# Attention with a routed expert layer: weight casts under one condition of two engines, staging block picked by register

## The chip, the cores and the metric

The kernel runs on one core of a Trainium2 chip. The metric is the device time of one execution in microseconds, as a median over runs. The engines are TensorE (PE, with its weight loads PEld), VectorE (DVE), ScalarE (ACT), GpSimd (POOL) and SyncE (SP). SP only issues transfers and conditions. A "q" behind an engine's name (SPq, ACTq, DVEq) means its sequencer: waits, branches, issues.

## The reference

```python
scores = scale * np.matmul(q, k.transpose(0, 1, 3, 2)) - np.log(S)      # 8 x 12 heads, 448 x 64
attn_out = np.matmul(1.0 / (1.0 + np.exp(-scores)), v)
x = attn_out.transpose(0, 2, 1, 3).reshape(B * S, H * D)                # 3584 tokens x 768
expert_idx = argmax(cosine(x, expert_emb) / tau)                         # 8 experts
for e in range(E):
    mask = expert_idx == e
    h = np.maximum(x[mask] @ w1[e], 0.0)                                 # 768 -> 1024
    out[mask] = gate_w[mask, None] * (h @ w2[e])                         # 1024 -> 768
```

Each token goes to one expert alone. How many tokens an expert gets is known only at run time.

## The kernel before, in words

The first part is attention over 48 head pairs, with the routing worked out beside it. The second part, which the change touches, is the expert layer. The tokens are sorted by expert into tiles of 128 rows, the fullest expert first. Two early tiles of that expert (-2 and -1) run ahead of the loop, which then goes over tiles `t = 0 ..`, at most `MAXL`; tiles past the last are skipped.

A tile has its rows gathered by POOL (`gather`, L1019) and transposed by a transfer of SP (`xt`, L1021). `layer1` is 36 matmuls against w1 (L200; L206 when the tile holds at most 64 tokens). `hidden` takes the result out on ACT (L259) and DVE (L261) and transposes it by two transfers of SP (`hT`, L263). `layer2` is 48 matmuls against w2 (L212; L219 for 64 tokens or fewer), `evac2` scales the output (L903, L905), and POOL scatters it (L1048). The loop runs `layer1` one tile ahead of `layer2`.

Weights come from memory in float32 and are used as two float16 parts. ACT writes the high part of a chunk (`high`, L160), DVE subtracts it from the float32 value for the low part (`low`, L164). w1 has 6 chunks of 128 x 1024, w2 has 8 of 128 x 768. There is one set of float16 tiles, `wts`. The float32 chunks lie in one of two stages, 0 or 1, by the expert's rank: the second expert uses stage 1, the third stage 0, and so on. The stages are separate tiles per chunk (`stages[stage][which][c]`); in the trace the first four w1 chunks of stage 0 are called `stage`, all others `s_w`.

`cast(u, which)` casts the weights if a new expert begins at tile `u`. The table `ci[:, 0]` holds 0 for no cast, 1 or 2 for a cast from stage 0 or 1. For ACT and then for DVE it goes through both stages, each under a condition of its own (L989), so there are two conditions on each engine in a call, ACT's for stage 1 standing ahead of DVE's for stage 0. w1 is cast two tiles ahead of the expert's first tile, behind `layer1(t + 1)`, w2 one tile ahead, behind `layer2(t)`. `fetch(u, n)` issues part `n` of 4 of the weights of the expert after next into the stage that `cast` has freed, again with one condition for each stage (L979), on SP. The calls for one expert are spread over four rounds of the loop, in the order in which SP issues transposes too.

Order: ACT, SP and POOL, and PE and DVE, keep the order of the program in the loop (`manual_schedule`). The last `hT` ahead of the loop, of tile -1, is the one that the planner places on SP by itself. The second expert's w1 (six transfers of 512 KB) is fetched beside the last two head pairs, its w2 ahead of and in round 0; the third expert's four parts are fetched in rounds 0, 0, 1 and 2.

```python
for en in (ET.Activation, ET.DVE):
    for st in range(2):
        with tc.If(regs[en, u] == 1 + st):
            weight_steps(None, which, range((NKC, NFC)[which]), st)[1 + (en == ET.DVE)]()
```

Of the kernel before, what the change touches and what calls it, by code (L numbers as in the profile page):

```python
# [12 lines left out]
F32 = mybir.dt.float32  # L13
I32 = mybir.dt.int32
AF = mybir.ActivationFunctionType
ALU = mybir.AluOpType
# [5 lines left out]
P = 128  # L22
# [7 lines left out]
E = 8  # L30
# [15 lines left out]
GC = P * JG  # L46
MAXL = (NT - (GS + 1) * GC // E + (E - 1) * (P - 1)) // P + 2
MINL = NJ - NE
# [58 lines left out]
def attn_moe_kernel(ctx: ExitStack, tc: tile.TileContext, q, k, v, emb, tau, w1, w2, consts, eye, out, dbg=None):  # L107
# [3 lines left out]
    dpool = ctx.enter_context(tc.tile_pool(name="dpool", bufs=1, space=DRAM))  # L111
    stg = ctx.enter_context(tc.tile_pool(name="stg", bufs=4))
    ps_s = ctx.enter_context(tc.tile_pool(name="ps_s", bufs=2, space=PSUM))
# [30 lines left out]

    stages = [[None] * 2, [None] * 2]

    def weight_steps(e, which, chunks, stage=None):
        src, w, i = (w1, F, 0) if which == 0 else (w2, DM, 2)
        tiles = [stg.tile([P, F], F32, name="stage")[:, :w] if stage is None else stages[stage][which][c] for c in chunks]

        def fetch():
            for c, s in zip(chunks, tiles):
                nc.sync.dma_start(s, src[bass.ds(e, 1), c * P:(c + 1) * P, :].rearrange("o p f -> (o p) f"))

        def high():
            for c, s in zip(chunks, tiles):
                if stage is None:
                    nc.vector.tensor_scalar(wts[i][:, c, :], s, SW, None, op0=ALU.mult)
                else:
                    nc.scalar.activation(wts[i][:, c, :], s, AF.Copy, scale=SW)  # L160

        def low():
            for c, s in zip(chunks, tiles):
                nc.vector.scalar_tensor_tensor(wts[i + 1][:, c, :], s, SW, wts[i][:, c, :], op0=ALU.mult, op1=ALU.subtract)  # L164

        return fetch, high, low
# [107 lines left out]
    with ExitStack() as actx:  # L274
# [271 lines left out]
        def choose(c):  # L546
# [19 lines left out]
            yield 1.0  # L566
            nc.vector.scalar_tensor_tensor(least, eoh, 2.0, eoh2, op0=ALU.mult, op1=ALU.add)
            nc.vector.scalar_tensor_tensor(rank0, least, 512.0, cs("desc"), op0=ALU.mult, op1=ALU.add)
# [111 lines left out]
        with tc.manual_schedule(engines={ET.SP, ET.PE, ET.Activation, ET.DVE, ET.Pool}):  # L680
            for i in range(NPAIR):
# [62 lines left out]
                if er:  # L744
                    while wq and len(wp) < 2 + 2 * (i + 6 > NPAIR):
                        fetch_next()
                    if i + 2 >= NPAIR:
                        for c in range(3 * (i + 2 - NPAIR), 3 * (i + 3 - NPAIR)):
                            weight_steps(er[1], 0, [c], 1)[0]()
                if i == 0:  # L750
# [6 lines left out]
                if i + 3 == NPAIR:  # L757
                    mctx.close()
                    ps_m.append(mctx.enter_context(tc.tile_pool(name="ps_m", bufs=2, space=PSUM)))
                    qctx.close()  # L760
                    bw = ctx2.enter_context(tc.tile_pool(name="bw", bufs=1, side="right", reuse_waits="tile"))
                    bp2 = ctx2.enter_context(tc.tile_pool(name="bp2", bufs=2, side="right", reuse_waits="tile"))
                    stages[1][0] = [bw.tile([P, F], F32, name=f"s1_w1_{c}") for c in range(NKC)]
                if i == 0:
# [151 lines left out]
    with tc.issue_after(six_op.ins):  # L916
# [24 lines left out]
        nc.vector.scalar_tensor_tensor(pr, pr, -2.0, kp[:, 1:], op0=ALU.mult, op1=ALU.add)  # L941
        to = bp1.tile([P, MAXL], F32, name="to")
        nc.vector.tensor_scalar(to, pr, 1.0, None, op0=ALU.add)
        vd = bp1.tile([P, MAXL], F32, name="vd")
# [9 lines left out]
        nc.vector.tensor_tensor(hm[:, NE:], hm[:, NE:], vd, op=ALU.mult)  # L954
        nc.vector.tensor_scalar(pr, hm[:, NE:], 2.0, -4.0, op0=ALU.mult, op1=ALU.add)
        nc.vector.tensor_tensor(pr, pr, vd, op=ALU.mult)
        ci = bp1.tile([P, 4, MAXL], I32, name="ci")
        nc.vector.tensor_scalar(ci[:, 2], pr, 4.0, None, op0=ALU.add)
        nc.vector.tensor_tensor(ci[:, 0], ca, to, op=ALU.mult)
        nc.vector.scalar_tensor_tensor(ch, nx, some[:, 0:1], ch, op0=ALU.is_lt, op1=ALU.mult)  # L960
        nc.vector.tensor_tensor(ci[:, 3], ch, to, op=ALU.mult)
        pos = bp1.tile([P, E], F32, name="pos")
# [8 lines left out]
    def fetch(u, n):  # L971
        if u and not 2 <= u < MAXL:
            return
        if u not in regs:
            regs[u] = (nc.values_load(ci[0:1, 3, u:u + 1], engines=[ET.SP], min_val=0, max_val=2),
                       nc.values_load(ci[0:1, 1, u:u + 1], engines=[ET.SP], min_val=0, max_val=E - 1))
        to, e = regs[u]
        for st in range(2):
            with tc.If(to == 1 + st):  # L979
                weight_steps(e, *PARTS[n], st)[0]()  # L980

    def cast(u, which):
        if not 2 <= u < MAXL:
            return
        for en in (ET.Activation, ET.DVE):
            if (en, u) not in regs:
                regs[en, u] = nc.values_load(ci[0:1, 0, u:u + 1], engines=[en], min_val=0, max_val=2)
            for st in range(2):
                with tc.If(regs[en, u] == 1 + st):  # L989
                    weight_steps(None, which, range((NKC, NFC)[which]), st)[1 + (en == ET.DVE)]()  # L990

# [3 lines left out]
    for w in wp:  # L995
        for f in w[1:]:
            f()
    man.enter_context(tc.manual_schedule(engines={ET.Activation, ET.SP, ET.Pool}))
    layer2_full([hT.pop((-2, half)) for half in range(2)], po[0])
    evac2(-2, po[0], bp1.tile([P, DM], F32, name="obe"))  # L1000
    rest = token_rest()
    next(rest)
    with tc.tile_pool(name="xr2", bufs=4, reuse_waits="tile") as xr2:
        nrm[:] = xr2, nc.vector
        for f in later:
            f()
    xctx.close()
    bp4 = ctx2.enter_context(tc.tile_pool(name="bp4", bufs=1, reuse_waits="tile"))
    stages[1][1] = [bp4.tile([P, DM], F32, name=f"s1_w2_{c}") for c in range(NFC)]
    stg2 = ctx2.enter_context(tc.tile_pool(name="stg2", bufs=1, reuse_waits="tile"))  # L1010
    stages[0] = [[stg.tile([P, F], F32, name="stage") for c in range(4)] + [stg2.tile([P, F], F32, name=f"s0_w1_{c}") for c in range(4, NKC)],
                 [stg2.tile([P, DM], F32, name=f"s0_w2_{c}") for c in range(NFC)]]
    bp3 = ctx2.enter_context(tc.tile_pool(name="bp3", bufs=3, reuse_waits="tile"))
# [28 lines left out]
    def scatter(t):  # L1042
# [3 lines left out]
        for d in range(2):  # L1046
            with (wide if d else guard)(ET.Pool, t):  # L1047
# [6 lines left out]
                stored.append(ins)  # L1054

    stored = []
    gather(0)
# [4 lines left out]
    for t in range(1, 3):  # L1062
        gather(t)
    layer1(0, xg_t.pop(0))
    weight_steps(er[1], *PARTS[2], 1)[0]()
    ends = ctx.enter_context(ExitStack())
    for t in range(MAXL):
# [9 lines left out]
        if t == 0:  # L1077
# [6 lines left out]
            nc.vector.memset(po[1][1], 0.0)  # L1084
            weight_steps(er[1], *PARTS[3], 1)[0]()
            fetch(0, 0)
        elif t < 3:
            fetch(0, 1 + t)
        if t > 1:
            fetch(t, 2)  # L1090
            fetch(t - 1, 3)
        cast(t + 2, 0)
        layer2(t)
        if t == 0:
            fetch(0, 1)
        fetch(t + 2, 0)
# [27 lines left out]
```

## Time and profile before

| | |
|---|---|
| median of 3 runs (lowest to highest) | 931.33 us (931.27 to 934.27) |
| the profiled execution, its own time | 925.67 us |
| span of the profile, first to last instruction | 923.8 us |
| PE busy in the span | 796.5 us (86%) |
| mean granted TensorE clock | 0.937 of full speed |

The profiled execution is 5.66 us shorter than the median; sums are made against it. In the lists of instructions a row gives start, duration, engine, source line, operation, tiles written and read, shape and count; in brackets stands how long the engine had been idle before, and what ended that.

### The profile page before, as it was taken

The page shows a single profiled execution, that of the slowest core. Times are in us where ns is not written, and L with a number is a line of the kernel's source. Part 1 is how long each engine was busy: PE and PEld are TensorE (multiplying, and loading weights), DVE is VectorE, ACT ScalarE, POOL GpSimd, SP SyncE. Part 2 cuts the span into 40 slices and gives each one's busy share as a digit, 9 for nine tenths or more (in the row PEclk, how much of TensorE's full clock was granted, in tenths as well). Part 3 has the DMA queues.
Part 4 walks back from the last instruction along what each step waited for, and adds up shares of the span by engine and source line. Part 5 has one row for each costly group of instructions (what it writes and reads, how often), then busy time and mean ns, then how long its engine had stood idle before and what let it go on. Part 6 is the DMA issues. An engine that isn't in the chain of part 4 may idle for free.

```text
span 923.8 us, 18744 instructions
## 1 busy us (share of the span) xinstructions
PE 796.5 (86%) x5847; PEld 382.5 (41%) x5847; DVE 372.7 (40%) x713; ACT 372.9 (40%) x551; POOL 198.1 (21%) x249
## 2 busy tenths in 40 slices
PE   6999999999998749987998998799995979566593
PEld 2344444444443325543454543355442435232351
DVE  3544575876784742201331112314323134303541
ACT  5777777777886030102221130313313213321530
POOL 2123523433431210311212110121120202011011
PEclk9999999999999979999999997899998889797798
DMA  8477979997987982976687655665788666677221
GB/s 209 116 174 179 239 182 235 272 233 202 217 237 168 225 177 44 294 212 157 181 213 165 133 114 144 180 199 114 190 205 179 145 208 166 174 170 157 60 49 41
DMA packets 243231, 160.80 MB, mean 174 GB/s; under 512 B 184748, under 2 KB 222102, under 8 KB 243024
## 3 DMA queue, kind: packets, MB, share of 16 engines
q1 hardware_dynamic: 233728, 123.29, 58.2%
q0 software_dynamic: 8880, 35.12, 11.9%
q8 instruction: 69, 1.13, 0.5%
q14 instruction: 138, 1.13, 0.4%
q10 hardware_dynamic: 416, 0.13, 0.1%
HBM read 96.69 MB, written 22.81 MB: 129 GB/s over the span
## 4 chain that ended last, share of the span: by engine, by line
issue 37%; DMA 13%; POOL 3%; POOLq 2%; another core or an unknown queue 0%
DMA xg<-xs,gix 9%; DMA out<-ob,six 4%; POOL xg L1019 2%; POOL out L1048 1%; POOLq L241 1%; POOLq L1047 0%; POOLq L1048 0%; POOLq L1018 0%; POOLq L1019 0%; POOLq L1069 0%; POOLq _compat.py:109 0%
## 5 line engine op out<-in xcount | busy, mean ns | idle before, releaser
L200 PE MATMUL pss<-w,xt 128*128 128x512 f16 x900 | 208.4, 390 | 37.0 <-DVEq L989 20.2
L212 PEld LDWEIGHTS <-hT 128*128 128x128 f16 x1296 | 132.6, 103 | 167.0 <-issue 52.2
L376 ACT ACTIVATE att<-pss,bias_s 128x896 f32<-128x896 f32 x144 | 139.8, 1005 | 32.0 <-PE pss L374 26.6
L200 PEld LDWEIGHTS <-xt 128*128 128x128 f16 x900 | 89.4, 100 | 150.2 <-issue 54.0
L1048 POOL DMA_INDIRECT out<-ob,six x58 | 58.6, 1010 | 433.7 <-ACTq L989 349.9
L212 PE MATMUL psa<-w,hT 128*128 128x384 f16 x624 | 114.2, 347 | 37.4 <-DMA hT<-hr 21.3
L212 PE MATMUL pso<-w,hT 128*128 128x384 f16 x672 | 122.3, 345 | 25.4 <-DVEq L989 11.9
L259 ACT ACTIVATE hr<-pss 128x512 f16<-128x512 f32 x60 | 35.4, 594 | 233.2 <-PE pss L200 155.1
L403 PE MATMUL psa<-att,vt 128*64 128x448 f32 x576 | 125.4, 556 | 0.0
L261 DVE SCALAR_TENSOR_TENSOR hr<-pss,hr 128x512 f16<-128x512 f32 x60 | 41.1, 689 | 197.4 <-ACT hr L259 180.1
L164 DVE SCALAR_TENSOR_TENSOR w<-s_w,w 128x768 f16<-128x768 f32 (+1 forms) x86 | 83.9, 1043 | 85.1 <-ACT w L160 62.0
L374 PE MATMUL pss<-kq 64*128 64x448 f16 x864 | 100.3, 356 | 2.2 <-ACT att L376 1.3
L160 ACT ACTIVATE w<-s_w 128x768 f16<-128x768 f32 (+1 forms) x86 | 70.9, 904 | 51.7 <-SPq L979 49.9
L341 POOL COPY pk<-qk 128x384 f32<-128x384 f32 x93 | 45.5, 516 | 141.9 <-PE ptr L353 75.4
L364 DVE SCALAR_TENSOR_TENSOR kq<-ptr,kq 128x448 f16<-128x448 f32 x96 | 59.8, 624 | 26.5 <-ACT kq L361 24.0
L374 PEld LDWEIGHTS <-kq 64*128 64x128 f16 x864 | 35.2, 95 | 75.6 <-issue 52.0
L363 DVE TENSOR_SCALAR kq<-ptr 128x448 f16<-128x448 f32 x70 | 43.4, 620 | 41.9 <-PE ptr L353 41.8
L403 PEld LDWEIGHTS psa<-att,vt 128*64 128x64 f32 x576 | 34.9, 136 | 60.7 <-issue 50.2
L428 DVE SCALAR_TENSOR_TENSOR xT<-psa,xT 128x384 f16<-128x384 f32 x96 | 32.9, 384 | 34.9 <-PE pss L374 25.7
L903 ACT ACTIVATE ob<-psa,own 128x384 f32<-128x384 f32 x16 | 9.3, 579 | 80.5 <-PE psa L212 62.4
L456 POOL TENSOR_TENSOR xf<-xrow 128x768 f32<-128x768 f16 x24 | 39.8, 1658 | 8.5 <-ACT xq L461 8.1
L164 DVE SCALAR_TENSOR_TENSOR w<-stage,w 128x1024 f16<-128x1024 f32 (+1 forms) x26 | 29.1, 1147 | 27.7 <-DMA xt<-xg 14.6
(212 smaller groups left out, 546.9 us busy)
## 6 DMA issues: line engine op xcount, KB each, us to landing
s_w<-in_moe_w SPq DMA_DIRECT2D x56, 384.0 KB
s_w<-in_moe_w SPq DMA_DIRECT2D x30, 512.0 KB
qk<-in_q SPq DMA_DIRECT2D x48, 192.0 KB
qk<-in_k SPq DMA_DIRECT2D x48, 192.0 KB
vt<-in_v SPq DMA_DIRECT2D x48, 192.0 KB
xs<-xrow POOLq DMA_DIRECT2D x24, 384.0 KB
stage<-in_moe_w SPq DMA_DIRECT2D x18, 512.0 KB
stage<-in_moe_w SPq DMA_DIRECT2D x8, 384.0 KB
```

Of the source, the lines that this page charges most:

```text
L160: nc.scalar.activation(wts[i][:, c, :], s, AF.Copy, scale=SW)
L164: nc.vector.scalar_tensor_tensor(wts[i + 1][:, c, :], s, SW, wts[i][:, c, :], op0=ALU.mult, op1=ALU.subtract)
L200: nc.tensor.matmul(ph[half][:, t % 2], xt[:, xi, kc, :], wts[wi][:, kc, half * HF:(half + 1) * HF], start=(n == 0), stop=(n == len(L1_TERM ...
L212: nc.tensor.matmul(po[d][:, :HD], hs[fc // 4][:, i, fc % 4, :], wts[wi][:, fc, d * HD:(d + 1) * HD], start=(n == 0), stop=(n == len(L2_TER ...
L261: d = nc.vector.scalar_tensor_tensor(hr[:, 1], ps, 0.0, hr[:, 0], op0=ALU.max, op1=ALU.subtract)
L341: en.tensor_copy(t.rearrange("p c h d -> p h c d"), qk[i][:, j])
L363: nc.vector.tensor_scalar(hi, x, SQK, None, op0=ALU.mult)
L364: nc.vector.scalar_tensor_tensor(lo, x, SQK, hi, op0=ALU.mult, op1=ALU.subtract)
L374: nc.tensor.matmul(ps[:, h, :S], x[r, ki, c * P:(c + 1) * P], x[r, qi, QC], start=(n == 0), stop=(n == 2))
L376: nc.scalar.activation(a, ps[:, :, :S], AF.Sigmoid, bias=bias_s, scale=1.0 / (8.0 * SQK * SQK))
L403: nc.tensor.matmul(accumulator(i)[h * D:(h + 1) * D, :S], vv[i][:, h, c, :], a[:, h, :], start=((i % 2 == 1 or i == 0) and c == 0), stop=( ...
L1048: ins = nc.gpsimd.indirect_dma_start(out.rearrange("n (h d) -> (n h) d", h=2), bass.IndirectOffsetOnAxis(ap=six[:, d, c:c + 1], axis=0), o ...
```

## The change

`cast` now has two conditions in a call, one for each half of the matrix's chunks, and each holds the work of both engines, ACT's and DVE's in turn chunk by chunk. The stage is no longer a Python constant with an arm for each value: both stages of a chunk are one tile `[P, 2, F]`, and the stage is an index in a register. `fetch` has one condition instead of two in the same way. The tables hold 2 for "nothing", 0 or 1 for the stage. The fullest expert gets at least 4 tiles in the loop instead of 2 (`LEAST`), and `MAXL` grows by 2. The fetch of the second expert's w1 leaves the end of the attention: its first part is issued on SP just ahead of `layer2(-2)`, the second ahead of `layer1(0)`, its w2 in rounds 0 and 1. The third expert's parts move to round 2 (parts 0 and 1), 3 and 4.

```diff
-MAXL = (NT - (GS + 1) * GC // E + (E - 1) * (P - 1)) // P + 2
+MAXL = (NT - (GS + 1) * GC // E + (E - 1) * (P - 1)) // P + LEAST      # LEAST = 4
+    def block(stage, which, c):
+        return stages[which][c][:, stage] if isinstance(stage, int) else stages[which][c][:, bass.ds(stage, 1)].rearrange("p o f -> p (o f)")
-                    if i + 2 >= NPAIR:
-                        for c in range(3 * (i + 2 - NPAIR), 3 * (i + 3 - NPAIR)):
-                            weight_steps(er[1], 0, [c], 1)[0]()
-                    stages[1][0] = [bw.tile([P, F], F32, name=f"s1_w1_{c}") for c in range(NKC)]
+                    stages[0][:3] = [bw.tile([P, 2, F], F32, name=f"s_w1_{c}") for c in range(3)]
...
     def fetch(u, n):
-        if u and not 2 <= u < MAXL:
+        if u and not LEAST <= u < MAXL:
...
-        for st in range(2):
-            with tc.If(to == 1 + st):
-                weight_steps(e, *PARTS[n], st)[0]()
+        with tc.If(to < 2):
+            weight_steps(e, *PARTS[n], nc.s_assert_within(to, 0, 1))[0]()
     def cast(u, which):
...
+        at, n = regs["c", u], (NKC, NFC)[which] // 2
+        for half in range(2):
+            with tc.If(at < 2):
+                now = nc.s_assert_within(at, 0, 1)
+                for c in range(half * n, half * n + n):
+                    for f in weight_steps(None, which, [c], now)[1:]:
+                        f()
...
     man.enter_context(tc.manual_schedule(engines={ET.Activation, ET.SP, ET.Pool}))
+    weight_steps(er[1], *PARTS[0], 1)[0]()
     layer2_full([hT.pop((-2, half)) for half in range(2)], po[0])
...
+    ahead(1)
     layer1(0, xg_t.pop(0))
-    weight_steps(er[1], *PARTS[2], 1)[0]()
...
-            weight_steps(er[1], *PARTS[3], 1)[0]()
-            fetch(0, 0)
-        elif t < 3:
-            fetch(0, 1 + t)
+        if t < 2:
+            ahead(2 + t)
+        elif t in (2, 4):
+            fetch(0, 0 if t == 2 else 3)
+        if t:
+            fetch(t, 2)
         if t > 1:
-            fetch(t, 2)
             fetch(t - 1, 3)
         cast(t + 2, 0)
         layer2(t)
-        if t == 0:
-            fetch(0, 1)
+        if t in (2, 3):
+            fetch(0, t - 1)
```

`ahead(n)` is `weight_steps(er[1], *PARTS[n], 1)[0]()`. The small table operations of VectorE ahead of the loop are rewritten for the new codes (two more of them).

## Rows read from the trace of the kernel before

**Rows 1.** Stretches with casts: busy time (PE, PEld, DVE, ACT, POOL), granted clock, DMA.

```profile
440.00:480.00 40.00, 37.88 (x215) 18.86 (x214) 15.08 (x19) 11.75 (x18) 8.15 (x8) 0.98 0.79 204
...
540.00:600.00 60.00, 47.54 (x233) 23.93 (x232) 19.32 (x22) 16.39 (x22) 6.66 (x7) 0.86 0.56 149
```

**Rows 2.** Waits of PE, whole span: sum in us, times, longest.

```profile
PE psa L212 <- DMA hT<-hr: 21.3, 3, 9.8
PE pss L200 <- DVEq L989: 20.2, 4, 6.6
```

**Rows 3.** Timeline of PE: two undisturbed layers, then six layers behind casts.

```profile
535.93 7.93 PE L200 MATMUL pss<-w,xt 128*128 128x512 f16 x36
543.70 7.96 PE L212 MATMUL psa<-w,hT 128*128 128x384 f16 x48
...
558.89 10.32 PE L200 MATMUL pss<-w,xt 128*128 128x512 f16 x35 [6.62 <-DVEq L989]
...
590.71 9.69 PE L212 MATMUL psa<-w,hT 128*128 128x384 f16 x46 [5.61 <-DVEq L989]
...
716.54 10.01 PE L200 MATMUL pss<-w,xt 128*128 128x512 f16 x35 [6.62 <-DVEq L989]
...
748.04 9.53 PE L212 MATMUL pso<-w,hT 128*128 128x384 f16 x46 [5.60 <-DVEq L989]
...
840.42 9.51 PE L200 MATMUL pss<-w,xt 128*128 128x512 f16 x35 [6.41 <-DVEq L989]
...
868.96 10.50 PE L212 MATMUL pso<-w,hT 128*128 128x384 f16 x46 [6.33 <-DVEq L989]
```

**Rows 4.** Timeline of ACT and DVE, the third expert's w1 (stage 0).

```profile
546.01 3.90 ACT L160 ACTIVATE w<-stage 128x1024 f16<-128x1024 f32 x4 [0.53 <-ACT hr L259]
...
551.88 4.63 DVE L164 SCALAR_TENSOR_TENSOR w<-stage,w 128x1024 f16<-128x1024 f32 x4 [5.50 <-ACTq L989]
```

**Rows 5.** Timeline of ACT, DVE and PE, the fourth expert's w1 (stage 1).

```profile
639.00 5.79 ACT L160 ACTIVATE w<-s_w 128x1024 f16<-128x1024 f32 x6 [1.52 <-SPq L979]
...
640.09 6.90 DVE L164 SCALAR_TENSOR_TENSOR w<-s_w,w 128x1024 f16<-128x1024 f32 x6 [1.88 <-ACT w L160]
...
643.28 8.23 PE L200 MATMUL pss<-w,xt 128*128 128x512 f16 x36
```

**Rows 6.** Waits of SP's own queue, whole span.

```profile
SPq L979 <- SPq L979: 87.8, 83, 5.7
```

**Rows 7.** The fetch conditions' line: its branches (ns min/median/max), who waited for it.

```profile
L979 SPq COMPARE_BRANCH  x268: 2/45/692, 382.2 to 917.7; - x134
...
  ACT w L160: 59.6, 10
```

**Rows 8.** Timeline of PE: two layers behind late casts.

```profile
800.49 0.80 PE L212 MATMUL psa<-w,hT 128*128 128x384 f16 x2 [10.31 <-ACT w L160]
...
833.43 0.58 PE L200 MATMUL pss<-w,xt 128*128 128x512 f16 x1 [9.93 <-ACTq L989]
```

**Rows 9.** Timeline of SP, end of attention; then PE, early tiles' second layers.

```profile
292.70 2.39 SPq L153 DMA_DIRECT2D s_w<-in_moe_w  x3
...
300.21 15.67 SPq L444 DMA_TRANSPOSE xrow<-xT  x4
...
325.09 9.72 PE L212 MATMUL psa<-w,hT 128*128 128x384 f16 x48 [8.11 <-DMA hT<-hr]
344.63 10.18 PE L212 MATMUL psa<-w,hT 128*128 128x384 f16 x48 [9.83 <-DMA hT<-hr]
```

**Rows 10.** Timeline of PE, rounds 2 to 5: the second expert's casts.

```profile
407.46 9.50 PE L212 MATMUL psa<-w,hT 128*128 128x384 f16 x48 [3.39 <-DMA hT<-hr]
...
423.12 9.65 PE L212 MATMUL pso<-w,hT 128*128 128x384 f16 x48 [2.15 <-DMA hT<-hr]
...
436.11 0.38 PE L200 MATMUL pss<-w,xt 128*128 128x512 f16 x1 [3.34 <-ACT w L160]
...
460.11 0.48 PE L212 MATMUL pso<-w,hT 128*128 128x384 f16 x2 [0.69 <-ACT w L160]
```

More of the change, by code (lines that the diff above doesn't have):

```diff
@@ L46 @@
 GC = P * JG
-MAXL = (NT - (GS + 1) * GC // E + (E - 1) * (P - 1)) // P + 2
+LEAST = 4
+MAXL = (NT - (GS + 1) * GC // E + (E - 1) * (P - 1)) // P + LEAST
 MINL = NJ - NE
@@ L111, in attn_moe_kernel @@
     dpool = ctx.enter_context(tc.tile_pool(name="dpool", bufs=1, space=DRAM))
-    stg = ctx.enter_context(tc.tile_pool(name="stg", bufs=4))
+    stg = ctx.enter_context(tc.tile_pool(name="stg", bufs=1))
     ps_s = ctx.enter_context(tc.tile_pool(name="ps_s", bufs=2, space=PSUM))
@@ L143, in attn_moe_kernel @@
     ident = cpool.tile([P, P], F32, name="ident")
-    stages = [[None] * 2, [None] * 2]
+    stages = [[None] * NKC, [None] * NFC]
+    stages[0][NKC - 2:] = [stg.tile([P, 2, F], F32, name=f"s_w1_{c}") for c in range(NKC - 2, NKC)]
+    halves = [t[:, i] for t in stages[0][NKC - 2:] for i in range(2)]
+    def block(stage, which, c):
+        return stages[which][c][:, stage] if isinstance(stage, int) else stages[which][c][:, bass.ds(stage, 1)].rearrange("p o f -> p (o f)")
     def weight_steps(e, which, chunks, stage=None):
         src, w, i = (w1, F, 0) if which == 0 else (w2, DM, 2)
-        tiles = [stg.tile([P, F], F32, name="stage")[:, :w] if stage is None else stages[stage][which][c] for c in chunks]
+        if stage is None:
+            tiles = [halves[0][:, :w] for c in chunks]
+            halves.append(halves.pop(0))
+        else:
+            tiles = [block(stage, which, c) for c in chunks]
         def fetch():
@@ L566, in choose @@
             yield 1.0
-            nc.vector.scalar_tensor_tensor(least, eoh, 2.0, eoh2, op0=ALU.mult, op1=ALU.add)
+            nc.vector.scalar_tensor_tensor(least, eoh, float(LEAST), eoh2, op0=ALU.mult, op1=ALU.add)
             nc.vector.scalar_tensor_tensor(rank0, least, 512.0, cs("desc"), op0=ALU.mult, op1=ALU.add)
@@ L941, in attn_moe_kernel @@
         nc.vector.scalar_tensor_tensor(pr, pr, -2.0, kp[:, 1:], op0=ALU.mult, op1=ALU.add)
-        to = bp1.tile([P, MAXL], F32, name="to")
-        nc.vector.tensor_scalar(to, pr, 1.0, None, op0=ALU.add)
+        nc.vector.tensor_scalar(pr, pr, -2.0, None, op0=ALU.add)
         vd = bp1.tile([P, MAXL], F32, name="vd")
@@ L954, in attn_moe_kernel @@
         nc.vector.tensor_tensor(hm[:, NE:], hm[:, NE:], vd, op=ALU.mult)
-        nc.vector.tensor_scalar(pr, hm[:, NE:], 2.0, -4.0, op0=ALU.mult, op1=ALU.add)
-        nc.vector.tensor_tensor(pr, pr, vd, op=ALU.mult)
         ci = bp1.tile([P, 4, MAXL], I32, name="ci")
-        nc.vector.tensor_scalar(ci[:, 2], pr, 4.0, None, op0=ALU.add)
-        nc.vector.tensor_tensor(ci[:, 0], ca, to, op=ALU.mult)
+        nc.vector.tensor_tensor(ca, ca, pr, op=ALU.mult)
+        nc.vector.tensor_scalar(ci[:, 0], ca, 2.0, None, op0=ALU.add)
+        nc.vector.tensor_scalar(ca, hm[:, NE:], 2.0, -4.0, op0=ALU.mult, op1=ALU.add)
+        nc.vector.tensor_tensor(ca, ca, vd, op=ALU.mult)
+        nc.vector.tensor_scalar(ci[:, 2], ca, 4.0, None, op0=ALU.add)
         nc.vector.scalar_tensor_tensor(ch, nx, some[:, 0:1], ch, op0=ALU.is_lt, op1=ALU.mult)
-        nc.vector.tensor_tensor(ci[:, 3], ch, to, op=ALU.mult)
+        nc.vector.tensor_tensor(ch, ch, pr, op=ALU.mult)
+        nc.vector.tensor_scalar(ci[:, 3], ch, 2.0, None, op0=ALU.add)
         pos = bp1.tile([P, E], F32, name="pos")
@@ L977, in fetch @@
         to, e = regs[u]
-        for st in range(2):
-            with tc.If(to == 1 + st):
-                weight_steps(e, *PARTS[n], st)[0]()
+        with tc.If(to < 2):
+            weight_steps(e, *PARTS[n], nc.s_assert_within(to, 0, 1))[0]()
     def cast(u, which):
-        if not 2 <= u < MAXL:
+        if not LEAST <= u < MAXL:
             return
[L985 to L990, printed above, removed]
+        if ("c", u) not in regs:
+            regs["c", u] = nc.values_load(ci[0:1, 0, u:u + 1], engines=[ET.Activation, ET.DVE], min_val=0, max_val=2)
+        at, n = regs["c", u], (NKC, NFC)[which] // 2
[5 more added lines that the diff above has]
+                        f()
     hidden(-1, 0)
@@ L1008, in attn_moe_kernel @@
     bp4 = ctx2.enter_context(tc.tile_pool(name="bp4", bufs=1, reuse_waits="tile"))
[L1009 to L1012, printed above, removed]
+    stages[0][3] = bp4.tile([P, 2, F], F32, name="s_w1_3")
+    stages[1] = [bp4.tile([P, 2, DM], F32, name=f"s_w2_{c}") for c in range(NFC)]
     bp3 = ctx2.enter_context(tc.tile_pool(name="bp3", bufs=3, reuse_waits="tile"))
@@ L1054, in scatter, with ahead @@
                 stored.append(ins)
+    def ahead(n):
+        weight_steps(er[1], *PARTS[n], 1)[0]()
     stored = []
```

## The prediction

> **What bounds the kernel now.** I read the stretches first, then the waits of PE, then the timelines of the engines at one cast. In the stretches the reader is to see that neither ACT nor DVE is short of time: in the 60 us around the third expert's casts DVE works 19.32 us and ACT 16.39 us, yet PE works only 47.54 us, at a granted clock of 0.86; around the second expert's casts PE works 37.88 of 40 us at 0.98 [rows 1]. So the loss goes by place, not by load. The waits of PE name two causes: transposes that land late, and DVEq at L989, which is the condition of the casts [rows 2]. The timeline of PE shows the latter as a pattern: six layers start behind a wait of 5.6 to 6.6 us, and each then runs slower than an undisturbed one [rows 3].
>
> The engines' timeline at one of them says why. The third expert's w1 comes from stage 0: ACT casts from 546.01 us, and DVE begins only at 551.88, released by ACTq at L989 [rows 4]. In the program ACT's arm for stage 1 stands between ACT's and DVE's arm for stage 0, so DVE must know that ACT has left it. The fourth expert's w1 comes from stage 1, whose arm is ACT's last: DVE begins 1.09 us behind ACT and follows chunk by chunk, and the layer behind it takes 8.23 us, 0.30 us over an undisturbed 7.93 [rows 3, 5]. Three experts (third, fifth, seventh) use stage 0, two casts each; these are the six.
>
> **The change part by part.** *One condition for both engines.* It removes the arm that stands between. Idle time of the six: 6.62 + 5.61 + 6.62 + 5.60 + 6.41 + 6.33 = 37.19 us [rows 3]. Slower running: 35 matmuls of w1 should take 35/36 of 7.93 = 7.71 us and took 10.32, 10.01 and 9.51 (2.61 + 2.30 + 1.80 over); 46 of w2 should take 46/48 of 7.96 = 7.63 us and took 9.69, 9.53 and 10.50 (2.06 + 1.90 + 2.87 over); together 13.54 us [rows 3]. What stays is what stage 1 shows: 0.3 us for w1 [rows 5], and for w2 about 1.2 us, from the 0.69 us before the second expert's w2 [rows 10] and as much again while it follows. 37.19 + 13.54 - 3 x 0.3 - 3 x 1.2 = 46.2, so **46 us** gained. Lower bound: if DVE had to wait for ACT's half (three of six chunks, half of about 5.8 us), it would begin 3 us earlier than now, six times: 18 us.
>
> *Register address and the count of conditions.* ACT and DVE pass as many conditions per tile as now (two halves for two stages), and the body exists once. The added address arithmetic is not in the trace for these engines; it lies beside a running cast of about 1 us a chunk (5.79 us for six [rows 5]), so I take 0; if it were not covered, 98 casts on each engine (7 experts of 14 chunks) at the 0.045 us of a branch [rows 7] are 4.4 us.
>
> *SP passes half as many conditions.* The arms not taken still count up semaphores, and SP waits in them: 87.8 us in 83 waits [rows 6]. Through these SP comes late to the point that frees a cast: ACT waited 59.6 us for it [rows 7], and PE lost 10.31 and 9.93 us in the worst two places, 3.34 us at the second expert's w1 [rows 8, 10]. Half of the arms go, but the next transfer waits too when the one before has not landed. Of these 23.6 us I take **9**; bounds 0 and 20. The Trainium skill (Advanced Engine Details and Errata, Control Flow Timing) puts a compare-and-branch at about 108 ns. By that the removed half of 134 conditions would be worth 7 us of SP's own time; the trace's branch takes 0.045 us [rows 7] and the waits are where the time is, so the sum goes by the waits.
>
> *The second expert's w1 leaves the attention.* Six transfers (3.1 MB) go out at 292.70 us and behind [rows 9]. Right behind them four transposes hold SP for 15.67 us, and PE waits 8.11 and 9.83 us for `hT`, then runs the two layers in 9.72 and 10.18 us instead of 7.96 [rows 3, 9]. Without the load the first wait should go; but half of it returns on SP ahead of the first gathers, the other half ahead of `layer1(0)`, and the planner may set `hT` of tile -1 behind it. Each half is 1.57 MB, 8 us of transfer at 204 GB/s [rows 1]. Bounds: a gain of 12, a loss of 10; I take a gain of **4**.
>
> *Rounds 0 to 2 lose the third expert's fetch.* There PE waits 3.39 and 2.15 us for `hT` and runs the layers in 9.50 and 9.65 us instead of 7.96, 8.8 us in all [rows 3, 10]. SP is freed of 17 conditions and four transfers there. I take **6**, bounds 0 and 8.8.
>
> *The third expert's fetch now lies just ahead of the second expert's casts, in the same tiles.* An index in a register can't be told from the other stage, so I expect a cast to wait for that fetch to land. 3.1 MB at 204 GB/s [rows 1] are 15 us. The first half's condition needs only the first part; the second starts some 4 us later than PE wants it. The same for w2. With the slower running behind a wait (about 2 us) I take a loss of **6**; bounds 0 (if they are told apart) and 20 (two waits of 8 us, 2 us each behind them). For later experts the fetch is rounds older than the cast.
>
> *`LEAST`, `MAXL`, table operations.* The second expert's w1 follows five loop tiles of the first, so a minimum of 4 adds none. The tables grow by 2 of 36 columns, and two small operations come in, all within PE's 8.11 us wait [rows 9]: 0; uncovered, under 1 us.
>
> **Sum:** 46 + 9 + 4 + 6 - 6 = 59 us. A PE that waits less meets SP and the transfers sooner: in the last tiles SP is late already [rows 8]. For that I take a sixth off, 10 us. 925.67 - 49 = 876.7 us for an execution like the profiled one; the median stands 5.66 us above it: **882 us**.
>
> **Rivals.**
> 1. *DVE follows only half by half.* If waits inside a shared condition are set for ACT's whole half, the 46 us become 18: 882 + 28 = 910 us. For it: DVE now waits on a condition's exit [rows 4]. Against it: inside one arm chunks are already told apart [rows 5].
> 2. *The merged tile makes late casts wait as well.* The seventh and sixth experts have few tiles, and their w2 could find the other stage's transfer unlanded: four waits of 8 us plus 2 to 2.5 of slow running instead of my 6: some 42, or 882 + 36 = 918 us. For it: SP is late there [rows 8]. Against it: DMA is only 56 to 79% busy [rows 1].
> 3. *Slower: a condition that two engines share makes them meet.* Four conditions a tile, 27 tiles: 108 meetings, each putting ACT's release of PE's results behind DVE. It undoes the gain of 49 us from 0.45 us each; at 0.6 us it would cost 65 us: 947 us. For it: `hidden` stands behind the casts on ACT. Against it: both engines are idle two thirds of the time [rows 1].
> 4. *Nothing moves*, because the moved fetches eat what the casts give: within 0.5% of 931.
>
> **How the numbers follow.** Forecast 0.72, first rival 0.10, second 0.07, third 0.07, fourth 0.04. The forecast's own range, from its bounds, is 860 to 904 us. Its upper side and the first rival together reach 914 us; below, SP's and the early stage's full bounds give 858. So 858 to 914. A measurement of this kernel tells about 0.5% from no change. Faster by more than that: 0.72 + 0.10 + 0.07 = 0.89; within it 0.04; slower 0.07.
>
> **What would show it.** Right: at the third expert's w1 DVE starts about 1 us behind ACT, and PE has no wait on DVEq at the cast's line anywhere; the layers behind the casts take 8 us again; SP's waits on itself fall well under 87.8 us. The merged tile shows as ACT or DVE waiting for `s_w` from memory at the second expert's casts, the half conditions as a gap after three or four chunks. The early stage: the four transposes of SP take half of 15.67 us and the 8.11 us wait shrinks. Wrong: if PE waits on the cast's line as before, the arm between was not the cause; if `hT` waits grow by as much as the cast waits fall, SP or the transfers have become the bound.

## The result, and the profile after

The changed kernel takes 845.19 us (median, 841.19 to 859.17), the kernel before 931.3 us in the same comparison: a ratio of 0.9104, 95% interval 0.903 to 0.9178. A second comparison gave 847.66 us and 0.9158 (0.9103 to 0.9213). So the change gains 78 to 86 us, where 49 were predicted, and the time lies below the range (858 to 914). The execution profiled beside the first result was a disturbed one, so the rows of after are those of the second comparison, whose profiled execution took 845.38 us (span 843.5).

In the changed kernel L163 issues a weight transfer, L986 is `fetch`'s condition, L996 `cast`'s, L170 and L174 the casts on ACT and DVE, L210 and L216 `layer1`, L222 and L229 `layer2`, L273 `hT`, L1030 `xt`. `psa` and `pso` are the two sets of tiles that `layer2` writes in turn. First the waits of PE (sum in us, times, longest):

```profile
PE psa L222 <- DMA hT<-hr: 13.2, 2, 11.4
PE pso L222 <- ACT w L170: 9.0, 1, 9.0
...
PE pss L210 <- DVE w L174: 6.4, 15, 0.9
...
PE pss L210 <- ACT w L170: 5.0, 3, 2.8
PE psa L222 <- ACT w L170: 3.4, 1, 3.4
```

No wait on DVEq is left, which was the second cause in [rows 2]. The stretches around the second and the third expert's casts, with the columns of [rows 1]:

```profile
418.00:458.00 40.00, 29.38 (x161) 14.46 (x161) 13.82 (x16) 11.30 (x16) 5.36 (x5) 0.87 0.89 241
525.00:585.00 60.00, 60.00 (x327) 31.82 (x325) 21.67 (x26) 18.64 (x26) 10.40 (x10) 1.00 0.72 181
```

Around the third expert PE now works without a gap at full clock. Around the second it works 29.38 of 40 us; the 37.88 of [rows 1] can't be held against that, because the two stretches do not hold the same layers. From the `layer2` of round 3 to that of round 5 it takes 447.22 - 407.13 = 40.1 us (rows below), before 460.11 - 423.12 = 37.0 [rows 10], so the place has got worse by 3.1 us. The timeline at the third expert's two casts answers to [rows 3, 4]:

```profile
530.54 5.79 ACT L170 ACTIVATE w<-s_w 128x1024 f16 x6 [0.88 <-DVE hr L271]
531.87 6.90 DVE L174 SCALAR_TENSOR_TENSOR w<-s_w,w 128x1024 f16<-128x1024 f16 x6 [1.36 <-ACT w L170]
535.92 7.93 PE L210 MATMUL pss<-w,xt 128*128 128x512 f16 x36
543.69 7.96 PE L222 MATMUL pso<-w,hT 128*128 128x384 f16 x48
...
553.74 5.98 ACT L170 ACTIVATE w<-s_w 128x768 f16 x8 [1.47 <-SPq L986]
554.62 7.04 DVE L174 SCALAR_TENSOR_TENSOR w<-s_w,w 128x768 f16<-128x768 f16 x8 [2.31 <-DMA hT<-hr]
559.26 7.96 PE L222 MATMUL psa<-w,hT 128*128 128x384 f16 x48
```

DVE starts 1.33 and 0.88 us behind ACT, and both layers run undisturbed. The timeline of PE at the places of [rows 8 to 10] and at the end:

```profile
316.56 7.97 PE L222 MATMUL psa<-w,hT 128*128 128x384 f16 x48 [1.84 <-DMA hT<-hr]
335.94 10.18 PE L222 MATMUL psa<-w,hT 128*128 128x384 f16 x48 [11.40 <-DMA hT<-hr]
...
395.23 7.96 PE L222 MATMUL psa<-w,hT 128*128 128x384 f16 x48
...
407.13 7.97 PE L222 MATMUL pso<-w,hT 128*128 128x384 f16 x48
...
447.22 0.80 PE L222 MATMUL pso<-w,hT 128*128 128x384 f16 x2 [9.01 <-ACT w L170]
...
743.72 0.80 PE L222 MATMUL psa<-w,hT 128*128 128x384 f16 x2 [3.40 <-ACT w L170]
...
768.73 0.38 PE L210 MATMUL pss<-w,xt 128*128 128x512 f16 x1 [1.86 <-ACT w L170]
```

Held against the same layers before, the lead is 325.09 - 316.56 = 8.5 us at the first early layer (2 of them stem from the attention, whose end differs by 6 us between two executions of the changed kernel), 407.46 - 395.23 = 12.2 and 423.12 - 407.13 = 16.0 in rounds 2 and 3, and 460.11 - 447.22 = 12.9 at the second expert's w2, where a part is lost again. At the sixth expert's w2 it is 800.49 - 743.72 = 56.8, at the seventh's w1 833.43 - 768.73 = 64.7 us. The first early wait, the six casts and the late casts all give something; the trace alone doesn't say which part of the change pays for which.

### The profile page after: what moved, and what is told of

It reads as the page before. It is cut to its first block, busy times and chain, and to the rows that moved or that the text cites. A ratio compares the mean times of both kernels' runs of the same rounds, so it can differ in the third digit from the quotient of the medians.

```text
span 857.3 us, 17937 instructions
## 1 busy us (share of the span) xinstructions
PE 784.9 (92%) x5847; PEld 379.5 (44%) x5847; DVE 372.3 (43%) x715; ACT 372.9 (43%) x551; POOL 200.5 (23%) x249
## 3 DMA queue, kind: packets, MB, share of 16 engines
q0 software_dynamic: 8880, 35.12, 12.9%
## 5 line engine op out<-in xcount | busy, mean ns | idle before, releaser
L210 PE MATMUL pss<-w,xt 128*128 128x512 f16 x900 | 205.3, 385 | 12.3 <-ACT w L170 6.5
L222 PEld LDWEIGHTS <-hT 128*128 128x128 f16 x1296 | 129.5, 101 | 132.4 <-DMA hT<-hr 28.4
L174 DVE SCALAR_TENSOR_TENSOR w<-s_w,w 128x768 f16<-128x768 f16 (+3 forms) x112 | 112.9, 1067 | 87.7 <-ACT w L170 83.0
L210 PEld LDWEIGHTS <-xt 128*128 128x128 f16 x900 | 88.6, 99 | 122.5 <-issue 23.8
L222 PE MATMUL pso<-w,hT 128*128 128x384 f16 x672 | 118.1, 338 | 22.0 <-ACT w L170 10.1
L222 PE MATMUL psa<-w,hT 128*128 128x384 f16 x624 | 108.1, 335 | 13.7 <-DMA hT<-hr 11.9
L170 ACT ACTIVATE w<-s_w 128x768 f16 (+1 forms) x98 | 82.9, 922 | 68.4 <-SPq L986 59.4
L1028 POOL DMA_INDIRECT xg<-xs,gix x31 | 32.3, 1041 | 25.4 <-issue 12.0
```

Source lines behind the costliest of these rows:

```text
L210: nc.tensor.matmul(ph[half][:, t % 2], xt[:, xi, kc, :], wts[wi][:, kc, half * HF:(half + 1) * HF], start=(n == 0), stop=(n == len(L1_TERM ...
L222: nc.tensor.matmul(po[d][:, :HD], hs[fc // 4][:, i, fc % 4, :], wts[wi][:, fc, d * HD:(d + 1) * HD], start=(n == 0), stop=(n == len(L2_TER ...
L1028: nc.gpsimd.indirect_dma_start(xg, None, xs, bass.IndirectOffsetOnAxis(ap=ix, axis=0))
```

## The experiments

Ratios are to the kernel before on the same chip, with 95% intervals; 0.01 of it is some 9.3 us.

| what runs | us | ratio |
|---|---|---|
| the change, second and third comparison | 847.66, 848.36 | 0.9158 (0.9103 to 0.9213), 0.9158 (0.9115 to 0.9201) |
| before, casts in one condition per stage | 906.07 | 0.9785 (0.9729 to 0.9841) |
| before, fetches moved | 932.5 | 1.007 (1.0033 to 1.0107) |
| change, SP's fetches in two arms | 899.24 | 0.9705 (0.9648 to 0.9762) |
| change, casts as before | 892.8 | 0.9646 (0.9607 to 0.9685) |
| change, casts and two arms as before | 925.47 | 1.0033 (0.9989 to 1.0076) |
| change, fetch in if and else | 853.5 | 0.9241 (0.9204 to 0.9278) |
| change, arm that is never true behind each fetch | 909.61 | 0.9854 (0.98 to 0.9907) |
| the same with one transfer in it | 865.6 | 0.9378 (0.9308 to 0.9449) |
| change, whole matrix in one condition | 846.49 | 0.9169 (0.9129 to 0.9209) |
| change, third expert's fetches one place earlier | 842.78 | 0.9121 (0.9043 to 0.92) |
| change, third expert's fetches as before | 841.05 | 0.908 (0.9027 to 0.9134) |
| change, tile -1's `hT` under the written order | 842.66 | 0.9101 (0.9033 to 0.9169) |
| both of these small repairs | 831.9 | 0.8956 (0.8899 to 0.9014) |

The theory after the result: the casts' term was right, and SP's arms were under-priced. The rivals: the casts bring more than their own waits; or the moved fetches do.

**The change once more.**

> The changed kernel once more. Theory: the profiled execution (859.17 us) was a disturbed one, and the median here is 845 to 851 us against 931 before, a gain of 80 to 86 us; in its profile the attention ends as early as before the change and PE waits some 55 us in all. Rival: the profiled execution is typical, 857 to 861 us, and the gain is 66 to 72 us.

The theory's number, 847.66 us. In its profile the attention ends 2 us earlier than in that of before, so no gain hides there.

**One condition alone, on the kernel before.**

```diff
-        for en in (ET.Activation, ET.DVE):
-            for st in range(2):
-                with tc.If(regs[en, u] == 1 + st):
+        for st in range(2):
+            with tc.If(regs["c", u] == 1 + st):      # ACT's and DVE's casts together
```

> The kernel before, with ACT's and DVE's casts in one condition for each stage (still two static stages, whole matrix, SP's fetches as before). Theory: this alone is the term of 46 us, 931 - 46 = 885 us (880 to 892); no wait of PE on DVEq is left. Rival 1: earlier casts free the stages earlier and the later experts' fetches move up too, so that the late waits on SP go as well: 931 - 46 - 20 = 865 us. Rival 2: PE then only waits for SP and transposes in place of the casts, and half of the 46 us is given back: 908 us.

906 us: 0.0215, or 20 us. The timeline of PE shows where the rest of 46 went:

```profile
557.42 7.71 PE L200 MATMUL pss<-w,xt 128*128 128x512 f16 x35 [2.18 <-DVEq L988]
...
630.72 9.99 PE L212 MATMUL pso<-w,hT 128*128 128x384 f16 x48 [6.10 <-DMA hT<-hr]
...
791.26 0.80 PE L212 MATMUL psa<-w,hT 128*128 128x384 f16 x2 [8.89 <-ACT w L160]
...
823.34 0.58 PE L200 MATMUL pss<-w,xt 128*128 128x512 f16 x1 [8.32 <-ACTq L988]
```

The wait of 6.62 us at the third expert's w1 [rows 3] is down to 2.18. But a wait of 6.10 us for a transpose stands where PE had none, and the waits at the late casts are nearly as long as they were (8.89 and 8.32 us against 10.31 and 9.93 [rows 8]). What SP did ahead of that transpose:

```profile
612.32 2.22 SPq L153 DMA_DIRECT2D s_w<-in_moe_w  x4
625.03 1.03 SPq L1022 DMA_TRANSPOSE xt<-xg  x1
626.18 4.87 SPq L263 DMA_TRANSPOSE hT<-hr  x2
```

Between 614.54 and 625.03 us SP issues nothing; in the trace it passes the branches and semaphore steps of `fetch` there (L979). So what is behind SP took the place of what was behind DVE, and the second rival holds.

**The moves alone, on the kernel before.** The second and third expert's fetches in the changed kernel's places, separate tiles.

```diff
-                        for c in range(3 * (i + 2 - NPAIR), 3 * (i + 3 - NPAIR)):
-                            weight_steps(er[1], 0, [c], 1)[0]()
+    weight_steps(er[1], *PARTS[0], 1)[0]()       # ahead of layer2(-2); PARTS[1] ahead of layer1(0)
...
+        if t < 2:
+            weight_steps(er[1], *PARTS[2 + t], 1)[0]()
+        elif t in (2, 4):
+            fetch(0, 0 if t == 2 else 3)
+        if t in (2, 3):                          # behind layer2(t)
+            fetch(0, t - 1)
```

> The kernel before, with the fetches of the second and third expert alone moved to the changed kernel's places (stages apart, casts and conditions as before). Theory: rounds 0 to 3 give 8.8 us and the first of the two waits for hT (8.1 us) goes, with its slower running 1.8 us: 931 - 8.8 - 9.9 = 912 us. Prediction's terms 4 + 6: 921 us. Rival: the second expert's casts meet the third expert's fetches and give 12 us back, 924 us; in separate tiles there is no reason for that beyond SP's queue.

Slower by 0.3 to 1.1%. The early gain is there, and is lost at the second expert's casts, although the stages are separate tiles. The timeline of SP and ACT there:

```profile
460.15 14.02 SPq L153 DMA_DIRECT2D s_w<-in_moe_w  x7
468.40 5.97 ACT L160 ACTIVATE w<-s_w 128x768 f16<-128x768 f32 x8 [25.52 <-SPq L976]
...
469.29 0.80 PE L212 MATMUL pso<-w,hT 128*128 128x384 f16 x2 [19.16 <-ACT w L160]
```

ACT is held by SP, which is still issuing later experts' weights and passing the conditions between them, and not by its own data. The prediction's reason for a loss at this place, the merged tile, isn't needed for it.

**SP's two arms, on the changed kernel.**

```diff
-        with tc.If(to < 2):
-            weight_steps(e, *PARTS[n], nc.s_assert_within(to, 0, 1))[0]()
+        for st in range(2):
+            with tc.If(to == st):
+                weight_steps(e, *PARTS[n], st)[0]()
```

> The changed kernel, with SP's fetches again in two conditions of a fixed stage each (tiles merged and casts as changed). Theory: the term of 9 us for SP's arms was too small, and the arms cost some 20 us: 847 + 20 = 867 us, with waits of ACT on SP at the late casts. Prediction's term: 847 + 9 = 856 us. Rival: with the casts in one condition SP has slack and the arms cost nothing: 847 us.

899 us: the arms cost 0.9705 - 0.9158 = 0.0547, 51 us, more than twice what even the theory said. The condition's line on SP (ns min, median, max; first and last start), first in the changed kernel:

```profile
L986 SPq EVENT_SEMAPHORE  x313: 3/17/720, 411.8 to 835.5; - x157
L986 SPq COMPARE_BRANCH  x138: 3/45/167, 405.9 to 835.1; - x138
```

Then with two arms:

```profile
L987 SPq EVENT_SEMAPHORE  x710: 2/17/715, 414.7 to 891.7; - x178
L987 SPq COMPARE_BRANCH  x252: 3/45/697, 412.0 to 891.2; - x126
```

A body that is passed over leaves a semaphore step (EVENT_SEMAPHORE) for each of its transfers. With one arm there are 313 steps and 138 branches, with two arms 710 steps and 252 branches (the kernel before had 268 branches [rows 7]): the steps more than double, the branches do not. What SP waits for, in the changed kernel and then with two arms (sum, times, longest):

```profile
SPq L1030 <- DMA xg<-xs,gix: 58.6, 13, 10.4
SPq L986 <- SPq L986: 51.6, 46, 3.4
```

```profile
SPq L987 <- SPq L987: 91.6, 75, 6.6
...
SPq L1031 <- DMA xg<-xs,gix: 34.9, 6, 10.2
```

Its waits on itself with two arms are as high as before the change (87.8 us in 83 waits [rows 6]). With one arm SP more often stands ready before the gathers (58.6 against 34.9 us waiting for them): it has slack. And the waits of ACT with two arms:

```profile
ACT w L170 <- SPq L987: 98.2, 13, 20.8
```

**Casts as before, and both as before, on the changed kernel.** The first takes the diff of `cast` back, with arms for stage 0 and 1; the second takes back `fetch`'s two arms as well.

> The changed kernel with the casts alone as before (for each engine an arm for each stage, four arms of a fixed stage; SP's fetches in one condition by register, places as changed). Theory: behind late fetches the casts' fault was partly hidden, so with SP free it costs its full 46 us: 847 + 46 = 893 us, with six waits of PE on DVEq of 5.6 to 6.6 us. Rival: it costs the 21 us that its repair gave on the kernel before: 868 us. Rival: SP's slack lets DVE begin in time and little is lost: 850 us.

> The changed kernel with both the casts and SP's fetches in arms of a fixed stage, as before; what stays of the change is the merged tiles, the moved fetches and the count of least tiles. Theory: these three give nothing or lose some us: 932 to 940 us (the moves alone gave 1.007 of before), so that casts and SP's arms together make the whole gain. Rival: the merged tiles and moves are worth 15 us in this setting: 912 us.

892.8 and 925.47 us: the theory's number in the first (893), and in the second no difference from before, which takes 923.91 us on that chip. The waits of PE with the casts as before:

```profile
PE pss L210 <- DVEq L996: 18.7, 3, 6.6
...
PE pso L222 <- DVEq L996: 11.9, 2, 6.3
...
PE psa L222 <- DVEq L996: 5.6, 1, 5.6
```

Six waits again, 36.2 us; the six of [rows 3] sum to 37.19. And what SP waits for there:

```profile
SPq L1027 <- DMA xg<-xs,gix: 91.8, 19, 10.2
```

The four kernels make a table of two by two. From neither to the new casts alone: 1.0033 - 0.9705 = 0.0328, 30 us. To one arm on SP alone: 1.0033 - 0.9646 = 0.0387, 36 us. To both: 1.0033 - 0.9158 = 0.0875, 81 us. Together they bring 0.016, 15 us, more than the sum of each alone; the four half widths, added as squares, leave 9 us of doubt on that.

Where these times lie is seen in the four profiled executions (us; PE's waits as sums over `layer1` and `layer2`, those on ACT with the ones on its condition, those on transposes being `hT`):

| casts, SP's arms | span | PE busy | granted clock | waits on ACT | on transposes | on DVEq |
|---|---|---|---|---|---|---|
| as before, two | 920.5 | 792.6 | 0.932 | 44.9 | 18.1 | 37.4 |
| as before, one | 891.0 | 784.5 | 0.948 | 24.8 | 19.7 | 36.2 |
| new, two | 898.8 | 795.6 | 0.947 | 40.9 | 30.1 | 0.3 |
| new, one | 843.5 | 777.8 | 0.971 | 17.4 | 16.9 | 0 |

The new casts alone take away the waits on DVEq, but the waits on transposes grow by 12 us. One arm on SP takes 20 to 24 us off the waits on ACT. Beside the new casts it takes off 13 us of waits on transposes too. PE's work is the same in all four, so less busy time is faster running: 8 us with the casts as before, 18 with the new ones.

**Fixed stages, but one exit.** What costs: the fixed stage, the branch, or the body that is passed over?

```diff
         with tc.If(to < 2):
-            weight_steps(e, *PARTS[n], nc.s_assert_within(to, 0, 1))[0]()
+            with tc.If(to < 1) as br:
+                weight_steps(e, *PARTS[n], 0)[0]()
+            with br.Else():
+                weight_steps(e, *PARTS[n], 1)[0]()
```

> The changed kernel, with SP's fetch in one condition around an if and else of a fixed stage each, in place of the register index. Theory: what costs 52 us in two separate arms is that the arm not taken waits for landings on transfer queues of its own; if and else share their queues and have one exit, so 845 to 852 us, although the stage is a constant again. Rival: the register index is what helps (fewer instructions, other tiles' waits): near 899 us. Rival: the number of branches costs: one more for each of some 30 fetches taken, at 0.045 us, is nothing, so this can't be told from the theory.

853.5 us, 1.5 above the theory's range: 0.0464 of the 0.0547 goes without any register index. The steps of the outer condition, with both arms in it:

```profile
L986 SPq EVENT_SEMAPHORE  x313: 3/17/502, 412.9 to 840.2; - x157
```

They are 313, as with the index, so the steps for both arms stand once. The index isn't what pays, but for the 0.0083 (8 us) that are left, which may be the index or noise.

**A body that is never entered.**

```diff
         with tc.If(to < 2):
             weight_steps(e, *PARTS[n], nc.s_assert_within(to, 0, 1))[0]()
+        with tc.If(to > 2):                         # never
+            weight_steps(e, *PARTS[n], 0)[0]()      # second kernel: the first chunk of the part alone
```

> The changed kernel, with a second condition behind each of SP's fetches that is never true and holds the same part of the weights in stage 0 (three or four transfers). Nothing more is moved or computed. Theory: a body that is passed over costs the landing of the last transfers on its queues, so this brings back what two arms cost: 890 to 905 us, with SP's waits on itself at 85 us or more and late casts again. Rival: two arms cost because the taken one is of a fixed stage, or by branches alone: at most 5 us, 847 to 853 us.

> The same, but the condition that is never true holds one transfer in place of three or four. Theory: what counts is how many of SP's transfer queues a body that is passed over has to see empty; with one of them it costs clearly less than the whole part: 855 to 875 us. Rival: it is the condition itself, with any transfer in it, so the same 890 to 905 us.

909.61 us, a little over the 905 of the theory, and 865.6 us, within its range. The line of the condition that is never true, with the whole part in it, and SP's waits there:

```profile
L988 SPq EVENT_SEMAPHORE  x397: 17/17/17, 412.1 to 902.4; - x199
L988 SPq COMPARE_BRANCH  x114: 45/45/53, 411.9 to 902.1; - x114
```

```profile
SPq L988 <- SPq L988: 105.4, 66, 7.2
```

The same with one transfer in it:

```profile
L988 SPq COMPARE_BRANCH  x114: 45/45/53, 412.1 to 854.1; - x114
L988 SPq EVENT_SEMAPHORE  x114: 17/17/17, 412.3 to 854.3; - x114
```

```profile
SPq L988 <- SPq L988: 19.2, 17, 3.8
```

With 397 steps the condition costs 0.0696 or 65 us, with 114 it costs 0.022 or 20 us. Both kernels have the same 114 branches. A branch's own record is 0.045 us, but the step behind it starts some 0.17 us after it (0.2 us in the second kernel's rows, at the first and at the last), so the branches are some 19 us of SP's time in either kernel, and may be most of the 20 us. The 45 us between the two go with the transfers in the body passed over. What their steps wait for is seen at one place of the first kernel, where four transfers go out and the body passed over stands right behind them:

```profile
L163 SPq DMA_DIRECT2D s_w<-in_moe_w x4: 342/342/355, 453.2 to 454.9; - x4
DMA to landing us min/median/max: 4.1/4.8/5.5
...
L988 SPq EVENT_SEMAPHORE  x4: 17/17/17, 459.5 to 460.6; - x4
L988 SPq COMPARE_BRANCH  x1: 45/45/45, 455.5 to 455.5; - x1
```

The branch falls at 455.5 us, but the four steps only between 459.5 and 460.6, as the transfers land: the last, issued at 454.9, some 5.5 us later. So a step here waits for an earlier transfer's landing, and where it stands counts as well as how many there are: this kernel has as many steps as the one with two arms (313 + 397 = 710), and takes 0.0149 or 14 us more. The likely reason, not tested apart, is that here such a body stands behind every fetch just issued. The Trainium skill (Advanced Engine Details and Errata, Control Flow Timing) gives a compare-and-branch some 108 ns; the trace has 45 for the record and some 170 to the step behind it, and at none of these figures do 114 branches explain 65 us.

**Halves or the whole matrix.**

```diff
-        at, n = regs["c", u], (NKC, NFC)[which] // 2
-        for half in range(2):
+        at, n = regs["c", u], (NKC, NFC)[which]
+        for half in range(1):
```

> The changed kernel, with the whole matrix of a cast in one condition in place of halves (half as many conditions on ACT and DVE). Theory: inside a condition DVE and PE follow chunk by chunk, so halves matter little: 845 to 852 us. The prediction's first rival (waits set for ACT's whole body) would make it 18 us and more slower: 865 us and above. If conditions on ACT and DVE cost as SP's do, it is faster by some us: 840.

846.49 us (0.9169), no difference. The count of ACT's and DVE's conditions costs nothing here, and DVE follows chunk by chunk in either: in this kernel it starts 1.09 us behind ACT at the third expert's w1.

**What the change left: the second expert's w2.** In the changed kernel PE waits 9.01 us there. One kernel issues the third expert's fetches one place earlier, another in the places of before:

```diff
+        elif t < 4:                   # one place earlier
+            fetch(0, 2 * t - 3)
...
+        if t in (1, 2):               # behind layer2(t)
+            fetch(0, 2 * t - 2)
```

> The changed kernel, with the third expert's four fetches each one place earlier (end of round 1, begin and end of round 2, begin of round 3), all landed before the second expert's casts want the tile. Theory: the waits at the second expert's casts (2 us at w1, 9 to 12 us at w2) are the merged tile's and go: 847 - 10 = 837 us, unless rounds 1 and 2 lose some of it to transposes behind the fetches (up to 8.8 us in the kernel before). Rival: the wait at w2 is the fourth expert's fetches on SP, and nothing changes: 847 us.

> The changed kernel, with the third expert's four fetches back in rounds 0 (two), 1 and 2; all else as changed. Prediction's terms (6 us gained in rounds 0 to 2, 6 lost at the second expert's casts): no difference, 847 us. Theory by the trace of the changed kernel: rounds 0 to 2 lose up to 8.8 us and the second expert's w2 gains 9 to 10, again within 3 us of 847. Rival: the transposes of the first rounds suffer more than that, and it is 855 us or above.

842.78 us (its interval overlaps the change's) and 841.05 us (0.908 against 0.9158 on the same chip, the intervals just overlapping). In both the wait of 9 us on ACT is gone; in the first PE waits 2.85 us for a transpose in its place and 3.08 on ACT at the second expert's w1; in the second 1.02 us on ACT are left, and 2.27 for a transpose come in in round 3. So moving the third expert's fetches to later rounds was no gain; it rather cost some 7 us.

**What the change left: tile -1.**

```diff
+    man.enter_context(tc.manual_schedule(engines={ET.Activation, ET.SP, ET.Pool}))
     hidden(-1, 1)
     for w in wp:
         for f in w[1:]:
             f()
-    man.enter_context(tc.manual_schedule(engines={ET.Activation, ET.SP, ET.Pool}))
```

> The changed kernel, with the last hidden half of tile -1 under the written order, so that on SP its transposes stand ahead of the second expert's first fetch and of the first three gathers' transposes. Theory: the 10 to 11 us that PE waits for hT of tile -1 are SP's order there; the wait falls to some 2 us and the slow layer behind it to 8 us: 847 - 10 = 837 us. Rival: the fetch, now later, meets the first rounds and the second expert's casts, and all is given back: 847 us.

842.66 us, not clear of the change. The theory was half right: the transposes now go out ahead of the gathers', yet the wait fell only from 11.40 to 8.14 us in the profiled execution. The timeline of PE:

```profile
336.90 9.45 PE L222 MATMUL psa<-w,hT 128*128 128x384 f16 x48 [8.14 <-DMA hT<-hr]
```

**Both together.**

> The changed kernel, for comparison on the same chip: 0.916 of before, 845 to 850 us.

> The changed kernel with both small repairs, tile -1's transposes under the written order and the third expert's fetches one place earlier. If their gains (about 0.5% each, neither clear of the interval) are real and apart: 838 us, ratio 0.906 of before. Rival: both only shift the same wait, 843 to 847 us.

831.9 us against 848.36 on the same chip, the intervals apart: this version beats both kernels, by 0.02 (19 us) the change and by 0.104 the kernel before. The timeline of PE at tile -1 and at the second expert's two casts:

```profile
335.14 9.60 PE L222 MATMUL psa<-w,hT 128*128 128x384 f16 x48 [4.29 <-DMA hT<-hr]
...
417.09 0.59 PE L210 MATMUL pss<-w,xt 128*128 128x512 f16 x1 [3.37 <-ACT w L170]
...
441.40 0.50 PE L222 MATMUL pso<-w,hT 128*128 128x384 f16 x2 [0.75 <-DMA hT<-hr]
```

The two waits that it is about have fallen from 11.40 to 4.29 us and from 9.01 to 0.75; at the second expert's w1 3.37 us have come in. Up to tile -1 this kernel is the one of the repair before, where the wait was 8.14 us: its size differs between executions.

## Why the prediction was right and wrong

**The arm between (46 us): right in mechanism, and in size once SP is free.** With SP's queue free it is 0.9646 - 0.9158 = 0.0488, 45 us, and PE shows the six waits or none. Without that the same edit brings 30 us, or 20 on the kernel before: the 46 us could be had only with SP's term.

**SP's conditions (9 us): the step that failed.** The term is worth 36 us alone and 51 beside the new casts, against bounds of 0 and 20. The prediction saw the 87.8 us of SP's waits [rows 6] and that arms passed over make them. It then priced them by the idle time that PE had visibly lost behind SP, 23.6 us at three late casts, and took 9 of that because "the next transfer waits too when the one before has not landed". SP does keep 51.6 us of waits on itself, but 36.2 us of them went, and PE's waits on ACT alone fell by 20 to 24 us (the table with four rows above), about all that the prediction had counted. Two more parts it put at nothing without a reason. The first is the slower running of PE behind such waits, which it did count for the casts: 8 us, and 18 beside the new casts. The second is the transposes that go out late behind SP: 13 us beside the new casts. With the casts as before these do not show, since PE then stands at DVE's condition for 37 us and SP catches up: SP stands ready before the gathers for 91.8 us there, with the new casts for 58.6. So PE's visible losses were no bound; SP's own 87.8 us would have been one that holds.

The branches were misread too, though the sum did not go by them: [rows 7] has 268 branches, not 134, and 138 are left. The 130 that went are some 22 us of SP's own time at the 0.17 us from a branch to the step behind it; the prediction's 0.045 us is the branch's record alone.

**"A sixth off, 10 us": wrong in sign.** The prediction reasoned that a PE that waits less meets SP sooner. That is what the new casts alone do. But the change frees SP as well, and the two together bring some 15 us more than the sum, with 9 us of doubt.

**The moves (4 + 6 - 6): near zero, as the sum said, by other reasons.** With casts and arms as before, all that is left of the change gives 1.0033. In the changed kernel the first early wait went (8.11 to 1.84 us, and the layer 9.72 to 7.97), the second stayed, and rounds 0 to 3 run clean (the two waits that the prediction puts in rounds 0 to 2 lie in rounds 2 and 3 [rows 10]). The loss at the second expert goes by where SP is in its program: ACT waits for SP there in separate tiles too. Of the merged tile, casts waiting for `s_w` from memory, only small waits show, at w1 (1.7 us the longest). `LEAST` and the table operations weren't tried alone.

**The register address (0) and the meeting of the engines (rival 3):** with half the conditions on ACT and DVE nothing changes, so the meetings cost nothing. The address does not show either: with it six casts of w1 take 5.79 us on ACT and 6.90 on DVE, as without it [rows 5]. Rival 1 falls with DVE's 0.88 to 1.33 us behind ACT. Of rival 2 the late casts show 3.40 and 1.86 us, where before they were 10.31 and 9.93 [rows 8].

**In sum**, in the two by two: 30 + 36 + 15, less 3 for what is left of the change, is 78 us, and 46 + 9 + 4 - 10 was 49. Against the terms SP is 27 over, the casts are 16 under, the rest of the change is 7 under, and 15 stands in place of -10, 25 over: the miss of 29. The split goes by the order: with SP's arms taken first, the casts are the 45 us above. The range's lower end mixes two times: 858 takes the bounds' 19 us off 876.7, the time of an execution like the profiled one; off the median's 882 it would be 863. The measured time lies below either.

**What stays open:** why PE still waits 4 to 8 us for the transposes of tile -1 when no fetch or gather stands ahead of them on SP, and whether the two small repairs bring more together (19 us) than apart (5 and 3 us); the half widths, added as squares, leave some 15 us of doubt on the difference.

## What to carry to other kernels

In this program a condition that isn't taken isn't free when its body holds transfers: count the transfers in all bodies passed over, not the branches alone, look at what is still in flight ahead of them, and give alternatives one exit (a register index, or if and else). Price a late queue by the queue's own waits, and count the slower running behind them; what the bottleneck engine shows as lost behind the queue is too little as long as another wait covers it. Two edits that free two queues which hide each other's lateness must be priced together.

## What the runs showed that was not expected

A body of three or four transfers that is never entered, 114 times on SP, made the kernel 65 us longer; with one transfer in it, 20 us. A cast whose data lay ready waited 25.52 us for SP to pass the conditions ahead of it in the program, in separate tiles too.
